# First two heads' rows scanned in place, a shorter warm-up, and a last pass with tokens on the result's partitions

## The chip, the cores and the metric

The kernel runs on one core of one Trainium2 chip. The metric is the device time of one execution in microseconds. Five engines have queues of their own: TensorE (PE in the profile, its weight loads PEld), VectorE (DVE), ScalarE (ACT), GpSimd (POOL) and SyncE (SP), which issues the kernel's DMAs.

## What is computed

Causal attention with forget gates over 4 sequences of 576 tokens and 8 heads of 64, then two pairs of dense layers with 512 inputs, 2048 hidden units and 512 outputs each:

```python
cum    = cumsum(log(clip(f, 1e-4, 1.0)))              # one row for each of 32 heads
scores = q @ k.T / 8 + cum[:, None] - cum[None, :]    # causal
x      = softmax(scores) @ v                          # heads side by side: 2304 x 512
x      = relu(x @ w_in1) ** 2 @ w_out1
out    = g(x @ w_in2) @ w_out2     # g(h) = h if h >= 1, 0 if h <= -1, else (h + 1)**2 / 4
```

All is float32. A value that goes through the fast products of TensorE is split in a high and a low part, and each wide product is made as three (high by high, high by low, low by high).

## The kernel before

**Tiling.** The 2304 tokens are cut into five blocks (`BLOCKS`): four of 512 tokens and a last one of 256. Block 0 holds the first 256 tokens (`HEAD`) of sequences 0 and 1, block 1 those of 2 and 3, blocks 2 to 4 the rest. Ten segments follow one another, a block by a pair of dense layers (`mo` 0 or 1). A segment has 16 steps (`NFC`), one for each 128 hidden units: `h_group` makes h (12 products), `act_group` the activation on ScalarE and VectorE and its split into `gh` and `gl`, and two steps later (`LAG`) `out_group` adds 12 products to four accumulators in PSUM, one for each 128 output units, with weights stationary and activations moving. So the results of a block come with output units on the partitions, and `finish` copies and stores them transposed (`outT`). The attention of a block runs between the steps of an earlier one; that of block 0 has nothing ahead of it.

**The start.** Attention of the first 256 tokens goes by groups of four heads (`Group`, `attention32`), four groups for block 0. Queries and keys of a group lie in one of two buffers `QK`, 64 rows for the 64 features of q and k. The gates ride along in the same product on more rows: row 64 holds `cum` on the side of the keys against a constant -8, row 65 holds `cum` on the side of the queries against a constant 8. `clear` fills these rows, `setup` loads `f` (L485), clips it (L488), takes the logarithm (L490) and scans it for all 32 heads at once (L491). Group 0 gets its two rows straight from the scan's result by two DMAs (`first_rows`, L507); other groups get them from a copy in DRAM, `cumd` (L503, L618). Group 0's queries and keys come in two loads of two heads each (L605). The scores `s` (L643) go to VectorE (mask and row minimum, `E`, L589), ScalarE (exponential, L650), any of three engines (division by the sum), TensorE (transposes `tr`, L682; products with v, `av`, L695) and into `x`. Before the first scores, `warm_up` issues `WARM` products of a constant tile that nobody reads (L542).

**Order of the work.** Every operation is declared with the engines that may run it, a cost for each and a due time; `Schedule` plays the program through with these costs, gives an operation with a choice to one engine, and writes the instructions in the order of the starts it found. It does so once for each entry of `WEIGHTS`, which makes an engine dearer in that choice, with refinements of the due times, and keeps the plan that ends first by its own costs. `QE`, `VE` and `RE` are the earliest times of the first loads of queries and keys, values and weights. So an edit of one operation can move others.

**Weights** of the dense layers come in a coded form, are decoded once by ScalarE, VectorE and GpSimd (`decode`, `w_decode`), split (`w_split`) and written to DRAM for the later blocks.

## Time and profile before

| | |
|---|---|
| median of 3 runs | 947.32 us (946.98 to 948.59) |
| profiled execution | 946.77 us |
| its span | 945.0 us |
| TensorE busy | 933.9 us (99%) |
| ScalarE busy | 638.2 us (68%) |
| VectorE busy | 585.9 us (62%) |
| GpSimd busy | 183.3 us (19%) |

The span runs from the first to the last instruction or transfer that the profiler saw; the time of an execution is some 1.8 us longer. Busy time of TensorE includes the warm-up and the pipelined ends of products, which overlap, so that consecutive products are best read by the distance of their starts.

### The profile page before, as it was taken

Reading aid. Unit: us, or ns where it says so; the run is one execution under the profiler, and the core shown is the slowest. Engines: PE = TensorE matmul, PEld = TensorE weight load, DVE = VectorE, ACT = ScalarE, POOL = GpSimd, SP = SyncE. Lnnn points to the kernel's source line nnn. Section 1 sums busy time; section 2 is a strip of 40 time slices with the busy share of each in tenths; the row PEclk is TensorE's granted clock in tenths of the full one; section 3 lists DMA queues with packets and bytes.
Section 4 is the critical chain, followed back from the end, with each engine's and each line's share of the span. In section 5 each row is a group of like instructions: output and inputs, shape, how many; then the busy total and the mean of one; then the engine's idle time right before and its main releaser. Section 6 shows DMA issues by size and latency. Waiting matters only on the chain.

```text
span 945.0 us, 14242 instructions
## 1 busy us (share of the span) xinstructions
PE 933.9 (99%) x4770; PEld 782.9 (83%) x4770; DVE 585.9 (62%) x1319; ACT 638.2 (68%) x1269; POOL 183.3 (19%) x323
## 2 busy tenths in 40 slices
PE   7999999999999999999999999999999999999998
PEld 5677778877888888888788887888888888889998
DVE  8899999899777659776777668775211132220032
ACT  7988889998887868776777677876523343334444
POOL 3300101324231322432223322321000000002200
PEclk9999999999999999999999999999999999999999
DMA  7799998997999997878789887986655555559993
GB/s 217 230 372 367 333 400 307 369 353 262 342 291 294 276 262 214 278 246 267 228 275 295 224 250 224 291 254 188 250 197 196 204 181 203 195 197 373 366 370 143
DMA packets 126105, 254.72 MB, mean 270 GB/s; under 512 B 89808, under 2 KB 90480, under 8 KB 104080
## 3 DMA queue, kind: packets, MB, share of 16 engines
q1 hardware_dynamic: 126032, 253.81, 80.7%
q8 instruction: 38, 0.62, 0.3%
q14 instruction: 35, 0.29, 0.1%
HBM read 194.35 MB, written 38.45 MB: 246 GB/s over the span
## 4 chain that ended last, share of the span: by engine, by line
PE 92%; DVE 3%; DMA 2%; ACT 1%; issue 1%; POOL 0%; SPq 0%; DVEq 0%; ACTq 0%; POOLq 0%
PE h L1042 40%; PE acc L1093 13%; PE acc L1095 13%; PE acc L1094 13%; PE av L866 4%; PE s L787 2%; PE s L788 2%; DMA PT<-PP 1%; DMA raw-2_209<-in_w_dram 1%; DMA out_dram<-o 1%; DVE PP L841 0%; PE s1q L643 0%; PE s7q L643 0%; PE s4q L643 0%; PE s5q L643 0%
## 5 line engine op out<-in xcount | busy, mean ns | idle before, releaser
L1042 PE MATMUL h<-x,whl 128*128 128x512 f32 (+1 forms) x1896 | 434.7, 372 | 0.4 <-DVE whl L1019 0.3
L1042 PEld LDWEIGHTS h<-x,whl 128*128 128x128 f32 x1896 | 325.0, 188 | 56.4 <-issue 3.0
L1093 PE MATMUL acc<-gh,whl 128*128 128x512 f32 (+1 forms) x640 | 239.2, 374 | 0.7 <-ACT o L570 0.7
L1095 PE MATMUL acc<-gl,whl 128*128 128x512 f32 (+1 forms) x640 | 236.8, 370 | 0.0
L1094 PE MATMUL acc<-gh,whl 128*128 128x512 f32 (+1 forms) x640 | 236.3, 369 | 0.0
L582 DVE TENSOR_TENSOR gl<-g,gh 128x512 fp32r<-128x512 f32 (+1 forms) x122 | 82.7, 678 | 123.3 <-PE acc L1095 82.7
L1095 PEld LDWEIGHTS acc<-gl,whl 128*128 128x128 f32 x640 | 120.5, 188 | 21.2 <-POOL gl L584 0.2
L1093 PEld LDWEIGHTS acc<-gh,whl 128*128 128x128 f32 x640 | 120.6, 188 | 18.8 <-ACT o L570 1.3
L1094 PEld LDWEIGHTS acc<-gh,whl 128*128 128x128 f32 x640 | 120.6, 188 | 15.6
L584 POOL TENSOR_TENSOR gl<-g,gh 128x512 fp32r<-128x512 f32 (+1 forms) x38 | 44.4, 1168 | 341.2 <-PE acc L1095 253.1
L1060 ACT ACTIVATE r<-h 128x512 f32<-128x512 f32 (+1 forms) x80 | 43.9, 549 | 86.8 <-PE h L1042 82.9
L1073 DVE SCALAR_TENSOR_TENSOR g<-r,h 128x512 f32<-128x512 f32 (+1 forms) x80 | 50.5, 631 | 80.5 <-ACT r L1071 80.2
L1069 ACT ACTIVATE r<-h,half 128x512 f32<-128x512 f32 (+1 forms) x80 | 51.1, 639 | 61.0 <-PE h L1042 60.5
L841 DVE SCALAR_TENSOR_TENSOR PP<-E,st,PP 128x512 f16<-128x512 f32 (+2 forms) x128 | 78.2, 645 | 10.4 <-ACT PP L837 9.3
L804 ACT ACTIVATE E<-E,st 64x320 f32<-64x320 f32 (+2 forms) x96 | 63.6, 662 | 26.2 <-DVE st L589 15.8
L589 DVE CUSTOM_DVE_ANT_0 E<-s,mask 128x288 f32<-128x288 f32 (+2 forms) x128 | 61.8, 500 | 24.2 <-PE s L788 15.8
L837 ACT ACTIVATE PP<-E,st 128x512 f16<-128x512 f32 (+2 forms) x128 | 68.6, 591 | 6.3 <-DVE st L811 5.7
L866 PEld LDWEIGHTS av<-pr,vt 128*128 128x128 f32 x288 | 53.5, 188 | 12.0 <-ACT r L1069 0.9
L866 PE MATMUL av<-pr,vt 128*128 128x320 f32 (+2 forms) x288 | 61.5, 285 | 0.5 <-DVE st L589 0.5
L570 ACT ACTIVATE gh<-g 128x512 fp32r<-128x512 f32 (+1 forms) x66 | 38.1, 577 | 30.7 <-DVE g L1073 30.4
L575 POOL TENSOR_SCALAR pr<-PT 128x640 fp32r<-128x640 f16 (+2 forms) x49 | 28.5, 583 | 125.9 <-PE av L866 91.1
L1071 ACT ACTIVATE r<-r 128x512 f32<-128x512 f32 (+1 forms) x80 | 46.9, 587 | 2.0
(250 smaller groups left out, 1112.0 us busy)
## 6 DMA issues: line engine op xcount, KB each, us to landing
whl<-scr SPq DMA_DIRECT2D x112, 1024.0 KB
raw<-in_w_dram SPq DMA_DIRECT2D x28, 1024.0 KB
scr<-whl SPq DMA_DIRECT2D x28, 1024.0 KB
in<-in_qkv_dram SPq DMA_DIRECT2D x32, 608.0 KB
whl<-scr SPq DMA_DIRECT2D x32, 512.0 KB
out_dram<-o SPq DMA_DIRECT2D x16, 256.0 KB
QK<-in_qkv_dram SPq DMA_DIRECT2D x7, 512.0 KB
raw<-in_w_dram SPq DMA_DIRECT2D x6, 512.0 KB
```

The source lines that it names most:

```text
L582: alts["DVE"] = (dve_t(n), lambda: nc.vector.tensor_sub(out(), a(), b()), True)
L589: return nc.vector.tensor_tensor_reduce(out=out, in0=ps, in1=mask[:m, OFF - q0:OFF - q0 + n], scale=scale, scalar=3e38, op0=ALU.add, op1=A ...
L804: nc.scalar.activation(Ec.tile[:m, :e], Ec.tile[:m, :e], AF.Exp, scale=-1.0, bias=nmx(), accum_out=st.tile[:m, 1, ci:ci + 1])))}, [*tops, ...
L837: nc.scalar.activation(hi, x, AF.Copy, scale=r())
L841: nc.vector.scalar_tensor_tensor(lo, x, r(), hi, op0=ALU.mult, op1=ALU.subtract)
L866: nc.tensor.matmul(av.tile[:, c0:W], vt.tile[:, kc, :, :], pr.tile[:, i, :n], start=(kc == 0 and i == 0), stop=(kc == NK - 1))
L1042: nc.tensor.matmul(ps.tile[:, :n], w.tile[:, 0, wi, kc * P:(kc + 1) * P], src.tile[:, kc, xi, :n], start=(kc == 0 and i == 0), stop=(kc == ...
L1069: o1 = sch.op(due, {"ACT": (act_t(n, True, 1), lambda: A.activation(r.tile[:, :n], ps(), AF.Relu, scale=0.5, bias=half))}, [o], [psb, r])
L1073: o2 = sch.op(due, {"DVE": (dve_t(n), lambda: v.scalar_tensor_tensor(g.tile[:, :n], r.tile[:, :n], 1.0, ps(), op0=ALU.min, op1=ALU.max))}, ...
L1093: nc.tensor.matmul(a.tile[:, :n], wh, gh.tile[:, :n], start=(fc == 0), stop=False)
L1094: nc.tensor.matmul(a.tile[:, :n], wl, gh.tile[:, :n], start=False, stop=False)
L1095: nc.tensor.matmul(a.tile[:, :n], wh, gl.tile[:, :n], start=False, stop=(fc == NFC - 1))
```

## The change

The diff has three parts.

1. `setup` loads the first 256 gates of heads 0 and 1 a second time, repeated on partitions 64 to 96 (33 partitions, both heads side by side), clips them and takes the logarithm there. `first_row` then scans a head's row on partition 64 and again on partition 96, straight into `QK`: four scans of 256 on VectorE in place of two of the four rows in each of the two DMAs. `first_rows` keeps its DMAs for heads 2 and 3. The second row of the gates moves from partition 65 to 96 for all groups. Clearing the second half of buffer 0 moves from VectorE to GpSimd, and the due time of filling `Q2` and `K2` goes from -30 to 30.
2. `WARM` goes from 17 to 12, the earliest times of the first loads move, and `WEIGHTS` has three entries instead of seven.
3. In the last 16 steps (block 4, second pair), `out_group` makes activations the stationary operand and weights the moving one: two accumulators of 128 tokens by 512 units, three products of 512 columns each, instead of four accumulators with three products of 256 columns. At the end each is copied in two halves and stored to `out4`, rows of tokens. The host joins the two outputs.

```diff
--- before.py
+++ after.py
@@ -46,15 +46,17 @@
 BASE = [sum(WIDTH[:i]) for i in range(len(BLOCKS))]
 OFF = 512
 QUAD = 4
+DIRECT = 2
+ROWS = (64, 96)
 SPARE = ("E", "g", "E", "o", "E", "r", "E", "g", "E", "o")
 
 SLAV = [0.0, 0.51, 0.75, 0.75, 0.0]
 SLQK = [0.0, 0.271, 0.412, 0.414, 0.0]
-QE = [0.0, 5.4, 8.66, 11.6]
-VE = [5.5, 6.1]
-RE = [1.36, 7.73, 16.0]
+QE = [0.0, 7.0, 8.66, 11.6]
+VE = [6.5, 7.6]
+RE = [2.4, 7.73, 16.0]
 LW = 29.1
-WARM = 17
+WARM = 12
 
 
 def pattern(bits):
@@ -120,7 +122,7 @@
 AHEAD = 0.30
 LEAD = 15.4
 
-WEIGHTS = [{}, *({"DVE": x, "POOL": x * y} for x in (0.4, 0.6, 0.8) for y in (0.0, 0.5, 1.0))]
+WEIGHTS = [{"DVE": x, "POOL": 0.0} for x in (0.6, 0.8, 1.0)]
 
 class Buf:
     def __init__(self, pool, make, kind=None):
...
@@ -476,21 +478,29 @@
     def setup():
         sb = new("x", "setup", [P, 2 * NKC * 512], F32)
         fr, lf, cum = (lambda i=i: sb.tile[:H * B, S * i:S * i + S] for i in range(3))
-        onesf = lambda: sb.tile[:H * B, 3 * S:4 * S]
+        onesf = lambda a=0, z=H * B, n=S: sb.tile[a:z, 3 * S:3 * S + n]
+        first = lambda a=ROWS[0], z=ROWS[1] + 1, c=0, m=DIRECT: sb.tile[a:z, 4 * S + HEAD * c:4 * S + HEAD * (c + m)]
         due = -100.0
         G, V_, A = nc.gpsimd, nc.vector, nc.scalar
         tiny_op.append(sch.op(due - 9, {"POOL": (0.05, lambda: G.memset(tiny, 2.0 ** -30))}))
         oh = sch.op(due - 200, {"POOL": (0.05, lambda: G.memset(warm, 0.5))})
         oh = sch.op(due - 200, {"ACT": (1.5, lambda: A.activation(warm, warm, AF.Ln))}, [oh])
+
+        b1 = sch.op(due - 2, {"SP": (dma_t(67584), lambda: nc.sync.dma_start(
+            out=first().rearrange("p (c n) -> p c n", n=HEAD),
+            in_=f[:DIRECT, :HEAD].partition_broadcast(ROWS[1] + 1 - ROWS[0])))}, [], [sb], early=0.0)
+        b2 = sch.op(due - 2, {"DVE": (0.37, lambda: V_.tensor_scalar(
+            first(), first(), 1e-4, 1.0, op0=ALU.max, op1=ALU.min))}, [b1], [sb])
+        b3 = sch.op(due - 2, {"ACT": (0.52, lambda: A.activation(first(), first(), AF.Ln))}, [b2, oh], [sb])
         o1 = sch.op(due, {"SP": (dma_t(73728), lambda: nc.sync.dma_start(out=fr(), in_=f))}, bufs=[sb], early=0.0)
-        o2 = sch.op(due - 5, {"POOL": (0.55, lambda: G.memset(onesf(), 1.0))}, bufs=[sb])
+        o2 = sch.op(due - 5, {"POOL": (0.55, lambda: G.memset(onesf(0, P), 1.0))}, bufs=[sb])
         sch.op(due + 90, {"POOL": (0.05, lambda: G.memset(half, 0.5))})
         o3 = sch.op(due, {"DVE": (0.37, lambda: V_.tensor_scalar(
             fr(), fr(), 1e-4, 1.0, op0=ALU.max, op1=ALU.min))}, [o1], [sb])
         o4 = sch.op(due, {"ACT": (0.58, lambda: A.activation(lf(), fr(), AF.Ln))}, [o3, oh], [sb])
         o5 = sch.op(-98.5, {"DVE": (0.67, lambda: V_.tensor_tensor_scan(
             cum(), onesf(), lf(), 0.0, op0=ALU.mult, op1=ALU.add))}, [o4, o2], [sb])
-        sch.op(due, {"ACT": (1.4, lambda: A.activation(warm, warm, AF.Exp))}, [o4])
+        sch.op(due, {"ACT": (1.4, lambda: A.activation(warm, warm, AF.Exp))}, [o4, b3])
         hi = lambda: fr().bitcast(F32R)
         lo = lambda: lf().bitcast(F32R)
         o6 = sch.op(T_START + 16, {
@@ -503,12 +513,17 @@
         o8 = sch.op(-98, {"SP": (dma_t(32768), lambda: nc.sync.dma_start(
             out=cumd, in_=cum()[:, :HEAD]))}, [o5], [sb])
 
+        def first_row(head, t, out, deps):
+            return sch.op((-101, -98.2)[head], {"DVE": (0.68, lambda: V_.tensor_tensor_scan(
+                out(), onesf(ROWS[t], ROWS[t] + 1, HEAD), first(ROWS[t], ROWS[t] + 1, head, 1), 0.0,
+                op0=ALU.mult, op1=ALU.add))}, [b3, o2, *deps], [sb, QK[0]])
+
         def first_rows(row, out, due, deps):
-            return sch.op(due, {"SP": (dma_t(4096), lambda: nc.sync.dma_start(
-                out=out(), in_=cum()[row:row + QUAD, :HEAD]))}, [o5, *deps], [sb, QK[0]], early=0.0)
+            return sch.op(due, {"SP": (dma_t(2048), lambda: nc.sync.dma_start(
+                out=out(), in_=cum()[row:row + QUAD - DIRECT, :HEAD]))}, [o5, *deps], [sb, QK[0]], early=0.0)
 
         zs = {}
-        due = -30.0
+        due = 30.0
         for i in range(2):
             for n, t in (("Q", Q2[i]), ("K", K2[i])):
                 z = None
@@ -528,9 +543,9 @@
         i2 = sch.op(-120, {"POOL": (0.3, lambda: G.affine_select(
             out=ident, in_=ident, pattern=[[-1, P]], compare_op=ALU.not_equal,
             fill=1.0, base=0, channel_multiplier=1))}, [i1])
-        return o7, zs, ms, i2, o8, first_rows
-
-    cum_op, zs, mask_op, id_op, cumd_op, first_rows = setup()
+        return o7, zs, ms, i2, o8, first_row, first_rows
+
+    cum_op, zs, mask_op, id_op, cumd_op, first_row, first_rows = setup()
     xb = {0: new("x", "x0")}
 
     def warm_up():
@@ -551,7 +566,7 @@
         rows = lambda a, z: QK[i].tile[a:z, n * half:n * half + n]
         kq = lambda a, z, t: rows(a, z).rearrange("p (c t n) -> p c t n", t=2, n=HEAD)[:, :, t, :]
         due = -98 + 2 * i + half
-        eng, m = ("POOL", nc.gpsimd) if i else ("DVE", nc.vector)
+        eng, m = ("POOL", nc.gpsimd) if i + half else ("DVE", nc.vector)
         fill = lambda out, x: {eng: (n / 1920 + 0.03, lambda: m.memset(out(), x))}
         kr = sch.op(due, fill(lambda: kq(D, P, 0), 8.0), [], [QK[i]])
         qr = sch.op(due, fill(lambda: kq(D, P, 1), 0.0), [], [QK[i]])
@@ -605,15 +620,18 @@
             loads.append(sch.op(g.due - 6, {"SP": (dma_t(P * n * 4 // parts), lambda c=c: nc.sync.dma_start(
                 out=reg()[:D, c], in_=src[:, c]))}, wait, [qk], early=QE[g.i] if g.i < len(QE) else None))
         row = g.b * H + g.h
-        place = lambda t, c0, c1: reg()[D + t:D + t + 1].rearrange("p (c t n) -> p c t n", t=2, n=HEAD)[:, c0:c1, t, :]
+        place = lambda t, c0, c1: reg()[ROWS[t]:ROWS[t] + 1].rearrange("p (c t n) -> p c t n", t=2, n=HEAD)[:, c0:c1, t, :]
         ready = []
         for i in range(parts):
             c0, c1 = QUAD * i // parts, QUAD * (i + 1) // parts
             if parts == 2:
-                if i == 0:
-                    rows = [first_rows(row, lambda t=t: place(t, 0, QUAD), -90, [*cleared[0, 0], *cleared[0, 1]])
+                for c in range(c0, min(c1, DIRECT)):
+                    ready.append([loads[i], *(first_row(
+                        c, t, lambda c=c, t=t: place(t, c, c + 1)[:, 0, :], cleared[0, i]) for t in range(2))])
+                if c1 > DIRECT:
+                    rows = [first_rows(row + DIRECT, lambda t=t: place(t, DIRECT, QUAD), -90, cleared[0, i])
                             for t in range(2)]
-                ready += [[loads[i], *rows]] * (c1 - c0)
+                    ready += [[loads[i], *rows]] * (c1 - DIRECT)
             else:
                 rows = [sch.op(g.due - 4, {"SP": (dma_t(4096), lambda t=t, c0=c0, c1=c1: nc.sync.dma_start(
                     out=place(t, c0, c1), in_=cumd[row + c0:row + c1, :].rearrange("(o c) n -> o c n", o=1)))},
@@ -1082,6 +1100,33 @@
         n = nb(s)
         w = whl[s]
         gh, gl, o3, o4 = gt.pop(s)
+        if s >= NS - NFC:
+
+            for d in range(n // P):
+                if fc == 0:
+                    accs[blk, mo, d] = new("acc", f"acc{blk}_{mo}_{d}")
+                    acc_op[blk, mo, d] = None
+                a = accs[blk, mo, d]
+
+                def mms(a=a, d=d):
+                    wh, wl = (w.tile[:, 1, i, :] for i in range(2))
+                    th, tl = (x.tile[:, d * P:(d + 1) * P] for x in (gh, gl))
+                    nc.tensor.matmul(a.tile, th, wh, start=(fc == 0), stop=False)
+                    nc.tensor.matmul(a.tile, th, wl, start=False, stop=False)
+                    nc.tensor.matmul(a.tile, tl, wh, start=False, stop=(fc == NFC - 1))
+
+                acc_op[blk, mo, d] = sch.op(
+                    when + 0.01 * d, {"PE": (3 * mm_t(DM), mms)}, [acc_op[blk, mo, d], o4, *whl_op[s]], [a, w, gh, gl])
+                if fc == NFC - 1:
+                    for i in range(2):
+                        z = slice(DM // 2 * i, DM // 2 * (i + 1))
+                        ob = new("E" if i else "o", f"o{blk}_{d}_{i}")
+                        o = sch.op(when - 4, copies(
+                            lambda ob=ob: ob.tile[:, :DM // 2], lambda a=a, z=z: a.tile[:, z], DM // 2, "ACT DVE", psum=True),
+                            [acc_op[blk, mo, d]], [a, ob])
+                        sch.op(when, {"SP": (dma_t(P * DM * 2), lambda ob=ob, z=z, d=d: nc.sync.dma_start(
+                            out=out4[d * P:(d + 1) * P, z], in_=ob.tile[:, :DM // 2]))}, [o], [ob])
+            return
         for d in range(NKC):
             if fc == 0:
                 accs[blk, mo, d] = new("acc", f"acc{blk}_{mo}_{d}")
...
```

## Rows read from the trace of the kernel before

**Rows 1.** The page, section 1: engine, busy us (share of span), instructions.
```profile
PE 933.9 (99%) x4770; PEld 782.9 (83%) x4770; DVE 585.9 (62%) x1319; ACT 638.2 (68%) x1269; POOL 183.3 (19%) x323
```

**Rows 2.** Busy time of each engine in stretches of the span.
```profile
core 0: us, PE busy (x) PEld busy (x) DVE busy (x) ACT busy (x) POOL busy (x), PEclk, DMA share, GB/s
...
48.00:100.00 52.00, 52.00 (x243) 41.11 (x241) 51.20 (x83) 45.48 (x76) 3.35 (x2) 1.00 0.99 377
...
300.00:600.00 300.00, 298.68 (x1438) 251.03 (x1437) 218.92 (x542) 223.30 (x467) 89.11 (x180) 1.00 0.84 253
```

**Rows 3.** Timeline from the start: start us, us, engine, line, operation [idle before].
```profile
0.74 0.41 SPq L485 DMA_DIRECT2D setup<-in_f_dram  x1
...
0.91 2.10 DVE L555 MEMSET QK<- 64x512 f32 x4 [0.91 <-PEq L1207]
...
1.39 5.41 PE L542 MATMUL warm<-ident 128*128 128x128 f32 x34 [1.39 <-POOL tiny L482]
...
3.04 0.45 DVE L488 TENSOR_SCALAR setup<-setup 32x576 f32<-32x576 f32 x1
3.52 0.68 ACT L490 ACTIVATE setup<-setup 32x576 f32<-32x576 f32 x1 [1.30 <-DVE setup L488]
...
4.82 1.35 DVE L491 TENSOR_TENSOR_SCAN setup<-setup 32x576 f32<-32x576 f32 x1
...
6.57 1.40 SPq L507 DMA_DIRECT2D QK<-setup  x2
...
7.72 0.66 ACT L963 ACTIVATE wf-2_238<-raw-2_209 128x512 f32<-128x512 f32 x1 [2.00 <-DMA raw-2_209<-in_w_dram]
...
9.21 2.86 PE L643 MATMUL s0q<-QK 128*128 128x128 f32 x16 [2.40 <-DMA QK<-setup]
```

**Rows 4.** Busy time around the first exponential, columns as in rows 2.
```profile
7.72:10.72 3.00, 1.51 (x10) 1.44 (x11) 2.44 (x8) 2.04 (x3) 0.68 (x3) 1.00 0.46 112
10.72:47.05 36.33, 33.92 (x211) 23.29 (x209) 30.37 (x134) 33.03 (x110) 10.14 (x17) 1.00 0.83 250
```

**Rows 5.** Chain that ended last: start us, us, what.
```profile
47.05 2.56 PE h L1042 x10
...
794.62 2.72 PE h L1042 x12
797.34 0.23 PE acc L1093
...
932.84 1.44 PE h L1042 x12
...
935.72 1.44 PE h L1042 x12
```

**Rows 6.** Timeline of the end, columns as in rows 3.
```profile
940.43 1.46 ACT L570 ACTIVATE o<-acc 128x256 f32<-128x256 f32 x4 [1.35 <-PE acc L1095]
...
940.84 1.80 SPq L1116 DMA_DIRECT2D out_dram<-o  x4
```

**Rows 7.** Stretches behind the last product, columns as in rows 2.
```profile
943.50:944.00 0.50, 0.00 (x0) 0.00 (x0) 0.00 (x0) 0.00 (x0) 0.00 (x0) 1.00 0.16 49
```

**Rows 8.** The page, section 5: a group of weight loads, busy us, mean ns, idle before.
```profile
L1093 PEld LDWEIGHTS acc<-gh,whl 128*128 128x128 f32 x640 | 120.6, 188 | 18.8 <-ACT o L570 1.3
```

**Rows 9.** Busy time in short stretches of the start, columns as in rows 2.
```profile
1.60:2.20 0.60, 0.60 (x4) 0.60 (x5) 0.55 (x2) 0.59 (x2) 0.53 (x2) 1.00 0.41 123
2.40:4.00 1.60, 1.60 (x9) 1.60 (x9) 1.35 (x4) 0.48 (x1) 1.50 (x3) 1.00 0.72 197
...
2.00:4.00 2.00, 2.00 (x11) 2.00 (x11) 1.75 (x4) 0.69 (x3) 1.83 (x4) 1.00 0.60 168
4.00:6.00 2.00, 2.00 (x19) 2.00 (x19) 1.80 (x3) 1.69 (x3) 1.93 (x5) 1.00 1.04 285
```

**Rows 10.** Instructions on the tile E0q: durations in ns (min/median/max), starts, shapes.
```profile
L589 DVE CUSTOM_DVE_ANT_0 E0q<-s0q,mask x8: 271/350/421, 10.4 to 12.5; 128x128 f32<-128x128 f32 x4, 128x256 f32<-128x256 f32 x4
L650 ACT ACTIVATE E0q<-E0q,st0q x8: 385/446/497, 10.7 to 14.8; 128x128 f32<-128x128 f32 x4, 128x256 f32<-128x256 f32 x4
```

More of the change, by code (lines that the diff above doesn't have):

```diff
@@ L380, in tile_attention_moe_moe @@
 @with_exitstack
-def tile_attention_moe_moe(ctx: ExitStack, tc: tile.TileContext, qkv, f, w2, outT):
+def tile_attention_moe_moe(ctx: ExitStack, tc: tile.TileContext, qkv, f, w2, outT, out4):
     nc = tc.nc
@@ L1212 @@
         args.append(nc.dram_tensor(f"in_{name}_dram", a.shape, _mybir.dt.from_np(a.dtype), kind="ExternalInput").ap())
-    outT = nc.dram_tensor("out_0_dram", (DM, NT), _mybir.dt.float32, kind="ExternalOutput").ap()
+    outT = nc.dram_tensor("out_0_dram", (DM, NT - WIDTH[-1]), _mybir.dt.float32, kind="ExternalOutput").ap()
+    out4 = nc.dram_tensor("out_1_dram", (WIDTH[-1], DM), _mybir.dt.float32, kind="ExternalOutput").ap()
     with _tile.TileContext(nc) as tc:
-        tile_attention_moe_moe(tc, *args, outT)
+        tile_attention_moe_moe(tc, *args, outT, out4)
     r = _run(nc, [arrays], core_ids=[0])
-    rows = r.results[0]["out_0_dram"].T
+    rows = _np.concatenate([r.results[0]["out_0_dram"].T, r.results[0]["out_1_dram"]])
     out = _np.empty(rows.shape, rows.dtype)
```

## The prediction

> **What bounds the kernel now.** I read the page first: TensorE is busy for 933.9 of the 945.0 us span [rows 1], so only 11.1 us are idle. Then stretches of the span: from 48 to 100 us TensorE is busy all 52.00 us, from 300 to 600 us for 298.68 of 300 us [rows 2]. What reaches the end from the middle is therefore the number and length of the products, which the change leaves alone up to the last pass. Two places are left: the start, before TensorE is always fed, and the end.
>
> At the start I read the timeline [rows 3]. Forgets `f` are loaded at 0.74 us, clipped at 3.04, logged at 3.52, scanned at 4.82; the sums go out by two DMAs at 6.57 us, and the first score product starts at 9.21 us after 2.40 us of waiting for them. Ahead of that stand 34 passes of warm-up (17 products, two passes each) from 1.39 to 6.80 us that compute nothing wanted. The page counts them as busy, so 5.41 us more of TensorE are free there than its share says.
>
> After the first product ScalarE is the fuller of the two engines around it: 33.03 of 36.33 us from its first exponential to 47.05 us, 91%, VectorE 30.37 us, 84% [rows 4]. From there on h products run without a break [rows 5]. At the end the steps follow one another without a gap, then come four copies, four stores and their data [rows 6, 7].
>
> **The change, part by part.**
>
> *Last pass.* A step of the last block is 2.88 us from one group of h products to the next (932.84 to 935.72 us [rows 5]); its 12 h products take 1.44 us, so the 12 output products, 256 columns each, take the other 1.44: 0.12 each. With 512 columns a product follows the one before after 0.227 us (12 h products in 2.72 us [rows 5]). The change makes the 12 of 256 columns into 6 of 512: 6 x 0.227 = 1.36 us, 0.08 less a step, and for 16 steps 1.28 us less. In rows, columns cost 0.107 us per 256, so 0.0133 us is the fixed part of each product, and six fixed parts go. The stationary operand is now the activations, the moving one the weights, both read as before; a weight load of 188 ns [rows 8] now lies beside 227 ns of product instead of 120.
>
> The Trainium skill, in "TensorE: Matmul & The Clock Gate", section "Back-to-back issue gap", gives a product its columns at 2.4 GHz and 2.5 ns on top, and by that the six saved would be worth 0.015 us a step, 0.24 us in all. The 0.0133 us of [rows 5] differ from it, and the trace decides.
>
> *The tail.* Before, four copies, 1.46 us in all, run on ScalarE as each accumulator ends [rows 6], the stores are issued from 940.84 to 942.64 us, and data flow until about 943.7 us [rows 7]. Afterwards two accumulators of 512 columns end 0.68 us apart (3 x 0.227), each with two copies and two stores of the same 128 KB. The last two stores become ready together instead of 0.36 us apart, and the queue issues them one behind the other; an issue takes about 0.40 us (1.80 us for four with their waits). The first store, too, starts about 0.4 us nearer to the end of the products (0.68 instead of 3 x 0.36 = 1.08 us ahead), and the same 512 KB still flow behind it. I charge one issue, 0.40 us; bounds are 0 and 0.80 (both copies on one engine). Last pass and tail: -1.28 + 0.40 = -0.88 us, between -1.28 and -0.48.
>
> *The first two heads.* A new load brings their rows to partitions 64 to 96, ahead of the old one. The old load's 72 KB moved between 1.6 and 2.2 us (123 GB/s for 0.6 us [rows 9]); the new one has 66 KB and the same place in the queue: landed at 2.4 us, at the latest 3.0, where the old clip started. A clip over 512 columns is 0.45 x 512/576 = 0.40 us, the logarithm 0.68 x 512/576 = 0.61 us [rows 3]; the old hops between these steps were 0.03 us and, behind a memset, up to 0.6. VectorE is free then: it clears three pieces instead of the first four before the old clip, so it is done at 0.91 + 3 x 0.53 = 2.4 us. The logarithm ends at 3.45 us. A scan of 256 is not in the trace. Below it is 1.35 x 256/576 = 0.60 us, above the whole 1.35; the mask pass of VectorE (0.28 for 128, 0.42 for 256 columns [rows 10]) shows a fixed part of some 0.13 us, so (1.35 - 0.13) x 256/576 + 0.13 = 0.67 us. Head 0 needs two: 3.55 + 1.34 = 4.9 us; no DMA follows, as they write the operand itself.
>
> *Warm-up.* Five products fewer are ten passes. From 2 to 4 us 11 passes touch the stretch, from 4 to 6 us 19 [rows 9]: about 0.21 us, then about 0.11 us each. The ten removed are of the fast kind, 1.1 us, so warm-up ends at 5.7 us. The load of queries and keys sits one issue (0.41 us) later; 197 GB/s from 2.4 to 4.0 us [rows 9] are 315 KB, enough for its 256 KB, so it lands near 4.4 us. The first product then starts at 5.7 us, set by the warm-up, not by the rows: 3.5 us earlier.
>
> *Heads 2 and 3* keep the old path: clip and logarithm right behind the new ones, long scan after head 0's at about 4.9, done at 6.3 us (7.6 if all four short scans go first), against 4.82 + 1.35 = 6.17. Their DMAs (two rows, not four) need the old 9.21 - 6.17 = 3.04 us from scan to product: 9.3 to 10.7 us. So two heads of the first four run in the gap, two come as before or up to 1.5 us later; queries of group 1, moved back to 7.0 us, queue behind these DMAs anyway. The delayed weights (1.36 to 2.4 us) are decoded by ScalarE from 7.72 us on [rows 3] and feed h products, which stand behind several groups of scores: nothing.
>
> *What of the 3.5 us passes.* The first exponential came 1.51 us after the first product (9.21 to 10.72 [rows 3, 10]), so it would come at 7.2 us. ScalarE then has its 33.03 us of work and the 2.04 us of decoding that stood ahead of it [rows 4] still before it: 35.07 us. At the old 91% this lasts to 45.8 us instead of 47.05, 1.3 us earlier; if VectorE takes the decoding, which the plan allows, the whole 3.5 us pass. VectorE has 16% free there, and gains only some 1.6 us of work (four scans 2.7, clip 0.4, less three memsets of 0.5). I take the middle, 2.4 us. From 48 us TensorE hands it on to the end unchanged [rows 2].
>
> Sum: -0.88 - 2.4 = -3.3 us. On the profiled execution, 946.77 us with a span of 945.0, that is a span of 941.7; the median of the runs is 947.32, 0.55 above that execution, so 944.0 us.
>
> **The rivals.**
>
> *All of it passes.* VectorE or GpSimd takes what ScalarE can't, 3.5 us, and the tail costs little: 947.3 - 3.5 - 0.9 = 942.9, with no tail loss 942.5. For it: 16% of VectorE is free. Against: only two heads are there to fill the gap, and each waits on its own chain.
>
> *The start's gain is swallowed.* Heads 2 and 3 come 1.5 us later and head 0's mask passes stand in VectorE's queue behind the long scan; the later weights and values cost waits, or the planner's new order, with VectorE priced higher, adds to the 1.4 us that TensorE now waits after 48 us. Then about 0.5 us is left of the start: 947.3 - 0.9 - 0.5 = 945.9, no measurable change. For it: VectorE is 98% busy from 48 to 100 us [rows 2]. Against: TensorE doesn't wait for it there.
>
> *TensorE's pace falls.* The granted clock reads 1.00 in each stretch here, yet the warm-up's pace doubled from one level to the other (1.2 to 2.4 GHz) only after about 3 us of products in a row [rows 9]. With a shorter warm-up and, behind it, two heads' products with gaps, the pace could drop back, and each microsecond of full-pace product then costs one more. It turns the sign of the result at 3.3 us and is measurably slower from 5.2 us; were it low from 5.7 to 16 us, it would cost about 6: 947.3 - 3.3 + 6 = 950. Against it: before, 2.40 us of idleness behind the warm-up did no harm (the 16 passes that follow took 2.86 us [rows 3]; eight of 128 and eight of 256 columns at the fast pace are 2.6), and the gap becomes shorter. The same page of the Trainium skill, Part 1, says that the slow level is the default, that activity lifts it and idleness brings it back; by this rule the danger is real, but the gap seen here didn't trigger it.
>
> *The last pass saves nothing.* Should the spacing of 0.227 us not hold with activations as the stationary operand (each set of weights in the array is now used for 512 columns once, and is itself the newest result of VectorE), the step stays at 2.88 us, the end is the added 0.40 us later, and the time is 947.3 - 2.4 + 0.4 = 945.3. Against it: h products of the same sizes keep 0.227 us for whole passes [rows 5]. The skill's figure above lies between this case and the forecast.
>
> **How the numbers follow.** The forecast, start 1.3 to 3.5 and end 0.5 to 1.3 us (942.5 to 945.4): 0.56. All passes, 942.7: 0.15. Swallowed, 945.9: 0.18. Pace falls, 950: 0.08. Last pass saves nothing, 945.3: 0.03. A measurement of this kernel tells some 0.2%, 1.9 us, from no change, so faster means under 945.4. Faster: 0.56 + 0.15 + 0.03 = 0.74; same 0.18; slower 0.08. The range leaves out the fallen pace and the best corner: 942.2 to 947.0; the likeliest case's own is 942.5 to 945.4.
>
> **What the profile will show.** The first score product near 5.7 us, without a wait for a DMA; four short scans of about 0.67 us; heads 2 and 3 at 9.3 to 10.7 us; 24 warm-up passes to about 5.7 us; the stretch where h products run without a break begins near 44.6 instead of 47.05 us; steps of 2.80 us in the last block, products 0.227 us apart; 0.4 us more from last product to end. The prediction is wrong if the first score waits for the queries' load or the clearing past 7 us, if ScalarE's share from the first exponential on falls below 85%, if new waits of TensorE above 2 us stand after 48 us, or if early passes run at 0.21 us again.

## The result, and the profile after

The changed kernel takes 953.83 us (952.36 to 956.25, 6 runs), the kernel before beside it 947.31 us (946.98 to 948.85, 6 runs): a ratio of 1.0069, with a 95% interval of 1.0058 to 1.0080. It is slower; the forecast was 944.0 us. The profiled execution took 952.79 us, with a span of 951.0 against 945.0 us.

The page, section 1, beside [rows 1]: TensorE has 0.4 us less to do and is idle for 17.5 instead of 11.1 us.

```profile
PE 933.5 (98%) x4664; PEld 778.0 (82%) x4664; DVE 596.1 (63%) x1323; ACT 631.6 (66%) x1263; POOL 186.6 (20%) x331
```

The timeline of the start, beside [rows 3]:

```profile
0.74 0.43 SPq L489 DMA_DIRECT2D setup<-in_f_dram  x1
...
1.39 5.46 PE L557 MATMUL warm<-ident 128*128 128x128 f32 x24 [1.39 <-POOL ident L543]
...
3.04 0.42 DVE L492 TENSOR_SCALAR setup<-setup 33x512 f32<-33x512 f32 x1
...
3.50 0.63 ACT L494 ACTIVATE setup<-setup 33x512 f32<-33x512 f32 x1 [1.27 <-DVE setup L492]
4.27 1.38 DVE L517 TENSOR_TENSOR_SCAN QK<-setup 1x256 f32<-1x256 f32 x2
...
5.69 1.35 DVE L501 TENSOR_TENSOR_SCAN setup<-setup 32x576 f32<-32x576 f32 x1
...
6.67 0.84 PE L661 MATMUL s0q<-QK 128*128 128x128 f32 x4
...
7.06 1.40 DVE L517 TENSOR_TENSOR_SCAN QK<-setup 1x256 f32<-1x256 f32 x2
...
8.52 0.92 PE L661 MATMUL s0q<-QK 128*128 128x128 f32 x4 [1.01 <-DVE QK L517]
...
8.83 0.40 ACT L668 ACTIVATE E0q<-E0q,st0q 128x128 f32<-128x128 f32 x1 [2.36 <-DVE st0q L604]
...
9.93 0.35 PE L661 MATMUL s0q<-QK 128*128 128x128 f32 x1 [0.49 <-DMA QK<-setup]
```

Head 0's rows need no DMA and its products start at 6.67 us, 2.54 us earlier than before. From 4.27 us on VectorE runs scan behind scan to 8.46 us, and head 1's products wait for its pair. The first mask (8.50 against 10.40 us) and the first exponential (8.83 against 10.72 us) are 1.9 us earlier, the first transposes 1.7 us (11.31 against 12.98 us). At the third group of transposes the lead is gone. The first line is from before, the others from after:

```profile
14.58 0.70 PE L682 MATMUL tr0q<-ident,E0q 128*128 128x128 f32 x3 [0.19 <-DVE E0q L674]
```

```profile
14.45 0.55 PE L700 MATMUL tr0q<-ident,E0q 128*128 128x128 f32 x3 [1.87 <-DVE E0q L692]
...
12.28 0.96 DVE L992 TENSOR_SCALAR low<-raw-2_212 128x512 uint16<-128x512 uint16 x1
13.14 0.48 DVE L675 TENSOR_SCALAR st0q<-st0q 128x2 f32<-128x2 f32 x1
...
12.57 0.35 POOL L532 MEMSET Q<- 64x320 f32 x1
12.90 0.70 POOL L539 TENSOR_SCALAR_AFFINE_SELECT mask<-mask 128x384 bf16<-128x384 bf16 x1
...
21.61 0.46 DVE L992 TENSOR_SCALAR low<-raw-1_270 128x512 uint16<-128x512 uint16 x1
```

TensorE waits 1.87 us for a division on VectorE that stands behind decoding. The decoding step ahead of it takes 0.96 us beside work of GpSimd; the same step takes 0.46 us at 21.61 us.

Stretches of the span, columns as in [rows 2]; the first answers to [rows 4]:

```profile
8.83:46.85 38.02, 32.98 (x212) 23.97 (x211) 35.89 (x140) 34.87 (x110) 6.01 (x14) 1.00 0.85 252
100.00:245.00 145.00, 143.18 (x666) 111.29 (x666) 140.37 (x229) 120.87 (x196) 27.75 (x27) 1.00 0.90 332
245.00:320.00 75.00, 72.42 (x348) 60.52 (x347) 54.61 (x137) 55.81 (x121) 19.78 (x44) 1.00 0.95 281
```

From the first exponential on, VectorE is busy for 35.89 of 38.02 us, 94% against 84%; ScalarE for 92% against 91%. None of VectorE's 5.5 us more is a scan, as those are over. Some 2 us each are divisions and decoding, and GpSimd has fewer of both (6.01 us busy against 10.14). The first output product starts at 49.79 us (before at 49.45). Then two stretches behind the start have idle TensorE, 1.82 and 2.58 us. They had none before:

```profile
100.00:245.00 145.00, 144.95 (x680) 114.39 (x679) 134.67 (x237) 128.86 (x210) 34.28 (x28) 1.00 0.90 334
245.00:320.00 75.00, 75.00 (x365) 63.19 (x364) 55.35 (x139) 60.07 (x126) 16.96 (x40) 1.00 0.99 303
```

In the first of them ScalarE is busy for 8.0 us less and VectorE for 5.7 us more: the change has no instruction there, but the planner drew engines and order anew. Most of the 5.7 us isn't added work. Summed over the instructions that ran more than 0.1 us longer than the median of their kind (line, tile and shape), VectorE took 12.4 us more than those medians there, against 6.7 us before. Each of them ran beside an instruction of GpSimd, which is busy for only 27.75 of the 145 us. One such, and the same step elsewhere:

```profile
105.38 3.33 DVE L1037 SCALAR_TENSOR_TENSOR whl<-wf,whl 128x1024 fp32r<-128x1024 f32 x1 [0.30 <-ACT whl L1034]
...
105.22 2.40 POOL L1002 TENSOR_TENSOR wf<-wf,low 128x1024 int32<-128x1024 int32 x1 [12.27 <-DVE wf L998]
...
158.07 1.23 DVE L1037 SCALAR_TENSOR_TENSOR whl<-wf,whl 128x1024 fp32r<-128x1024 f32 x1
```

TensorE's longest waits from 100 to 320 us in the trace of after (us, times, longest):

```profile
PE h L1060 <- DVE whl L1037: 1.1, 1, 1.1
PE acc L1138 <- ACT o L585: 1.1, 1, 1.1
PE s L805 <- DVE st L604: 1.0, 1, 1.0
```

The end, beside [rows 5, 6]: two lines of the chain, then the timeline of ScalarE's and SP's last work.

```profile
938.63 1.43 PE h L1060 x12
...
941.45 1.43 PE h L1060 x12
```

```profile
946.34 1.34 ACT L585 ACTIVATE o<-acc 128x256 f32<-128x256 f32 x4 [1.54 <-PE acc L1116]
...
946.75 1.81 SPq L1127 DMA_DIRECT2D out_dram<-o  x4
```

A step is 2.82 us (2.88 before). From the start of the last product (946.60 us; before 941.00) to the end of the span go 4.41 us, against 3.98.

Theory at this point: the last pass does about what was forecast; the start's lead dies in VectorE's queue; the new order costs the rest. Rivals: TensorE's pace, the stores, and GpSimd holding up VectorE's instructions. The last of these got no run of its own; what the traces show of it is told where it stands.

### The profile page after: what moved, and what is told of

Same layout as the page of the kernel before. It is cut to its first block, busy times and chain, and to the rows that moved or that the text cites. A ratio compares the mean times of both kernels' runs of the same rounds, so it can differ in the third digit from the quotient of the medians.

```text
span 951.0 us, 14066 instructions
## 1 busy us (share of the span) xinstructions
PE 933.5 (98%) x4664; PEld 778.0 (82%) x4664; DVE 596.1 (63%) x1323; ACT 631.6 (66%) x1263; POOL 186.6 (20%) x331
## 4 chain that ended last, share of the span: by engine, by line
PE 67%; DMA 2%; DVE 1%; ACT 1%; issue 0%; SPq 0%; ACTq 0%; DVEq 0%
PE h L1060 30%; PE acc L1138 10%; PE acc L1140 9%; PE acc L1139 9%; PE av L884 3%; PE s L805 2%; PE s L806 2%; DMA out_dram<-o 1%; PE acc L1114 1%; PE acc L1115 1%; PE acc L1116 1%; DMA in<-in_qkv_dram 0%; ACT PP L855 0%; DMA PT<-PP 0%; SPq L866 0%
## 5 line engine op out<-in xcount | busy, mean ns | idle before, releaser
L1138 PE MATMUL acc<-gh,whl 128*128 128x512 f32 (+1 forms) x576 | 220.9, 384 | 2.7 <-ACT o L585 2.7
L1140 PE MATMUL acc<-gl,whl 128*128 128x512 f32 (+1 forms) x576 | 218.7, 380 | 0.0
L1139 PE MATMUL acc<-gh,whl 128*128 128x512 f32 (+1 forms) x576 | 218.1, 379 | 0.0
L1140 PEld LDWEIGHTS acc<-gl,whl 128*128 128x128 f32 x576 | 108.4, 188 | 21.1 <-POOL gl L599 0.2
L1138 PEld LDWEIGHTS acc<-gh,whl 128*128 128x128 f32 x576 | 108.5, 188 | 20.3 <-ACT o L585 3.2
L1139 PEld LDWEIGHTS acc<-gh,whl 128*128 128x128 f32 x576 | 108.5, 188 | 15.6
L599 POOL TENSOR_TENSOR gl<-g,gh 128x512 fp32r<-128x512 f32 (+1 forms) x40 | 48.4, 1210 | 297.3 <-PE acc L1140 214.5
L590 POOL TENSOR_SCALAR pr<-PT 128x640 fp32r<-128x640 f16 (+2 forms) x55 | 33.5, 613 | 130.2 <-PE av L884 83.0
```

The lines of the kernel that those rows point to most:

```text
L1138: nc.tensor.matmul(a.tile[:, :n], wh, gh.tile[:, :n], start=(fc == 0), stop=False)
L1139: nc.tensor.matmul(a.tile[:, :n], wl, gh.tile[:, :n], start=False, stop=False)
L1140: nc.tensor.matmul(a.tile[:, :n], wh, gl.tile[:, :n], start=False, stop=(fc == NFC - 1))
```

## The experiments

In most kernels below the planner is replaced by a record of the engine and start that it gave each operation. "The old order" is the record of the kernel before: new operations are put in beside the ones that they replace, so a part can be measured without the planner's answer to it. Lateness, worked out from the traces, is the start of the first activation of a step on ScalarE minus that of the kernel before (us; segments and steps count from 0, two segments to a block); the last column is the difference of the spans:

```
segment, step                 0, 0    0, 4    2, 1    3, 0    5, 0    span
kernel before, starts        44.46   61.43  246.94  353.24  571.01   945.0
changed kernel               +1.27   +2.22   +3.22   +6.34   +6.18    +6.0
last pass, old order         +0.15   +0.15   +0.18   +1.02   +0.95    +0.4
start, old order             +3.37   +3.35   +3.41   +4.08   +4.52    +4.5
  + 14 filling products      +1.78   +1.76   +1.89   +3.66   +2.35    +2.2
  + fills off VectorE        +0.65   +1.60   +1.71   +1.61   +0.88    +1.1
  + decoding later           +2.09   +2.79   +2.80   +3.72   +3.37    +3.4
12 warm-up, old order        +0.96   +0.94   +0.96   +1.47   +2.71    +2.7
new start, old order behind  +1.63   +2.21   +2.18   +3.42   +4.57    +4.2
old start, new order behind  +1.33   +3.95   +4.45   +9.29   +8.26    +7.6
before, later plan           +0.06   +1.05   -1.55   +1.48   +2.15    +2.8
```

In the rows of the old order a lateness stays within 0.13 us from the fifth step (61 us) to 247 us. Ahead of that it can grow, by up to 0.95 us. In a new order the table also counts work that was moved from one step to another, so there TensorE's idle time says more.

### The last pass alone

The old order with the last pass of the change and nothing else of it; the diff is the hunks on `s >= NS - NFC` and `out4`.

> The last pass alone, every other operation on the engine and in the order of the kernel before. Order theory (the loss comes from the new order that the planner draws for everything behind the start): 946.4 to 946.9 us, 0.5 to 0.9 less than before. Start theory (the loss comes from the new work at the start itself): the same. If the swapped operands cost something: 947.3 or more.

947.04 us, 1.0005 [0.9996, 1.0013] (median, ratio to before, 95% interval): no difference that can be measured. Either theory expected 946.4 to 946.9. In the profile the lateness falls from 0.97 us at the last segment's first step to 0.41 at the end. So the part is worth some 0.56 us, less than the runs of one kernel differ (here those of before from 945.7 to 949.1).

### The start alone

The old order with the other hunks (load, clip, logarithm, scans, row 96, 12 warm-up products), without the last pass. The old order's places serve:

```diff
+            sch.put(("DVE", PLAN[8][1] - 0.004 + 0.001 * t + 0.006 * head))
             return sch.op((-101, -98.2)[head], {"DVE": (0.68, lambda: V_.tensor_tensor_scan(
```

> The new load, logarithm and scans for heads 0 and 1 and 12 warm-up products, the last pass as before, every other operation on the engine and in the order of the kernel before. Order theory: 945 to 947.5 us. Start theory: 951 us or more, since the four scans, the clip, the logarithm and the load are all there.

951.56 us, 1.0051 [1.0038, 1.0065]. The start itself is 3.4 us late, and TensorE hands that on unchanged to 247 us. VectorE (first fence) puts filling and decoding ahead of head 0's masks, which start 1.9 us later than before; unlike in the changed kernel, where they start 1.9 us earlier. TensorE then waits 3.79 us for the first transposes, and the granted clock (column PEclk of the second fence) is at the lower of its two levels, 1.2 GHz, when they come:

```profile
6.68 1.40 DVE L583 TENSOR_TENSOR_SCAN QK<-setup 1x256 f32<-1x256 f32 x2
8.25 2.36 DVE L599 MEMSET K<- 64x576 f32 x4 [0.18 <-issue]
...
12.28 0.28 DVE L670 CUSTOM_DVE_ANT_0 E0q<-s0q,mask 128x128 f32<-128x128 f32 x1
```

```profile
12.00:14.00 2.00, 0.00 (x0) 0.00 (x0) 2.00 (x14) 1.39 (x7) 0.00 (x0) 0.87 1.01 253
14.00:16.00 2.00, 1.14 (x5) 0.83 (x6) 1.86 (x14) 1.89 (x8) 0.48 (x1) 0.50 1.13 367
16.00:18.00 2.00, 2.00 (x10) 0.90 (x9) 1.31 (x7) 1.94 (x7) 0.00 (x0) 0.50 0.98 194
18.00:20.00 2.00, 2.00 (x10) 0.95 (x6) 0.28 (x1) 0.51 (x1) 0.00 (x0) 0.50 1.00 282
```

### Pace: filling products, and a shorter warm-up by itself

To the start alone, 14 products of the constant tile that nobody reads, behind head 0's scores:

```diff
+    def keep_busy(n):
+        ps = new("ps", "busy")
...
+                nc.tensor.matmul(ps.tile[:, :P], ident, ident, start=True, stop=True)
...
+    keep_busy(14)
```

> As f2_start (951.6 us), with 14 more products that nobody reads behind the first scores, in the 3.8 us in which TensorE waited there. If f2_start lost by the pace that fell in this gap: granted clock 1.00 from 8 to 48 us and 947 to 949 us. If the extra work on VectorE made the loss: 951 us or more.

949.41 us, 1.0024 [1.0014, 1.0034]: 2.2 us above before instead of 4.65, and just above the 947 to 949 expected from pace alone. The masks come when they came without the filling (12.3 us) and the transposes too (14.86 us), but at full clock:

```profile
14.00:16.00 2.00, 1.23 (x7) 0.64 (x7) 1.86 (x14) 2.00 (x9) 0.48 (x1) 1.00 1.16 363
16.00:18.00 2.00, 1.82 (x12) 0.91 (x11) 1.56 (x7) 1.89 (x8) 0.00 (x0) 1.00 0.86 177
```

The kernel before with the warm-up alone shortened:

```diff
-WARM = 17
+WARM = 12
```

> The kernel before on its own engines and in its own order, with 12 warm-up products instead of 17 and nothing else changed. If the five products hold TensorE's pace up through the wait for the first scores: the clock falls near 9 to 13 us and the time is 948 to 950 us. If they do nothing: 946.9 us.

948.37 us, 1.0011 [1.0002, 1.0020]. The first score products start at 9.21 us as before, behind an idle stretch that is no longer (2.32 against 2.40 us), but the 16 passes take 4.14 instead of 2.86 us [rows 3], at the lower clock; timeline, then stretches:

```profile
9.21 4.14 PE L704 MATMUL s0q<-QK 128*128 128x128 f32 x16 [2.32 <-DMA QK<-setup]
```

```profile
10.00:12.00 2.00, 2.00 (x10) 1.77 (x9) 1.46 (x9) 1.40 (x7) 0.00 (x0) 0.65 0.90 211
12.00:14.00 2.00, 1.76 (x7) 1.04 (x6) 1.51 (x11) 1.34 (x6) 0.48 (x1) 0.50 1.00 325
```

The whole change with its own order, but 17 warm-up products:

> The changed kernel in its own order on every engine, with 17 warm-up products instead of 12. If the shorter warm-up lets TensorE's pace fall in part of the runs (mean granted clock 0.998 in three of six, those 2 to 3 us longer): no run under 0.9995, median 952 to 952.8 us. If the warm-up has nothing to do with it: 953.8 us and the same spread.

952.88 us, 1.0063 [1.0051, 1.0076], not told apart from the changed kernel. The longer warm-up doesn't bring the time back in that order. It doesn't rule a lower pace out in every run: two of the five have a mean clock of 0.997.

### VectorE's queue at the start

To the kernel with 14 filling products, the constant fills of the second buffers K and Q on GpSimd:

```diff
+                    sch.put(("POOL", sch.take(1)[0][1] + 30.0))
                     z = sch.op(due, {
```

> The order of the kernel before, the new start without the last pass, the 14 filling products ahead of the first transpose of weights, and the constant fills of the second K and Q buffers moved from VectorE to GpSimd. Theory, VectorE's queue holds the start up once the pace is right: the first masks of head 0 come some 2 us earlier and the time is 946.5 to 948 us. Rival, VectorE's queue is no limit: no change from the kernel with the 14 products alone, 949.4 us.

948.64 us, 1.0014 [1.0006, 1.0023]: 1.7 us above before, and above the theory's 946.5 to 948. The masks start at 10.07 us, 2.2 us earlier; beside its own runs of before the time is 0.45 us less than with the filling alone, within the intervals. That doesn't speak against VectorE's queue. At the first step this kernel is 1.13 us ahead of the one with the filling alone, and by the third it has lost 0.95 us again. TensorE waits there for weights `whl` from VectorE, 1.26 instead of 0.35 us, and three steps of VectorE ahead of them take 0.13, 0.46 and 0.36 us longer while GpSimd does the fills that were moved to it. Two of the three, with the filling alone and with the fills moved:

```profile
45.27 0.44 DVE L573 CAST setup<-setup 32x576 fp32r<-32x576 f32 x1
46.97 0.68 DVE L1076 TENSOR_SCALAR wf<-wf 128x1024 int32<-128x1024 int32 x1
```

```profile
44.30 0.90 DVE L573 CAST setup<-setup 32x576 fp32r<-32x576 f32 x1
46.43 1.04 DVE L1077 TENSOR_SCALAR wf<-wf 128x1024 int32<-128x1024 int32 x1
```

Two kernels bring heads 0 and 1 forward in the queues of VectorE, ScalarE and GpSimd: the first has no filling products and 3 us of shift, the second 6 of them and 2.2 us.

```diff
+                    sch.shift = -3.0 if c + a < DIRECT else 0.0
```

> As f2_start, but the work of heads 0 and 1 behind the scores is put 3 us earlier in every queue, ahead of the decoding of the first weights, and the fills of Q2 and K2 leave VectorE. If f2_start lost because head 0's mask passes stood behind fills and decoding in VectorE's queue, and TensorE's pace fell in the gap that this left: 945 to 948 us, and a granted clock of 1.00 from 8 to 48 us. If the scans themselves, 2.8 us of VectorE, are the loss: 950 us or more.

> As the kernel with the fills moved, with 6 filling products, and the work of heads 0 and 1 on VectorE, ScalarE and GpSimd placed 2.2 us earlier in these engines' queues. Theory, order in VectorE's queue and TensorE's pace are all that the new start loses: the first step of the first block stands level with before or ahead of it, and the time is 945.5 to 948 us. Rival, the start has another limit (ScalarE's exponentials, the transfers of heads 2 and 3): the first step stays 1 us or more late and the time is 948.5 us or more.

951.74 us, 1.0050 [1.0036, 1.0063], and 953.33 us, 1.0064 [1.0048, 1.0080]. Both miss. In the first, without filling, TensorE is idle from 10 to 12 us and the granted clock is 0.50 from 14 to 16 us. In the second, score products wait 4.1 us for mask passes that stand behind decoding and divisions in the mixed order, and the granted clock is 0.50 from 10 to 16 us: neither says anything about VectorE. So the last one, with 5 filling products, moves only the five decoding instructions: in the record those on ScalarE go from 6.96 and 7.72 to 11.95 and 11.96 us of the plan, those on VectorE from 7.57, 8.47 and 8.93 to 13.00, 13.01 and 14.96.

> As the kernel with the fills moved to GpSimd (order of the kernel before, new start, no last pass), but the decoding of the first step's weights, three instructions on VectorE and two on ScalarE, is placed behind head 0's mask passes and first exponentials instead of ahead of them; 5 filling products instead of 14. Theory, VectorE's queue ahead of head 0's masks swallows what the earlier score products bring: the first mask comes near 8.1 us instead of 10.07, the first step of the first block 1 us or more earlier than with the fills moved alone, ahead of the kernel before, and the time is 946 to 948 us. Rival, behind the masks something else is due at the old time (the values' transfers, the weights): the first step is not earlier, and the time stays at 948.6 us or is longer.

950.39 us, 1.0034 [1.0021, 1.0048]: the masks start as the theory said, the time doesn't follow. The tile E0q of the kernels with fills moved and with decoding moved (ns min/median/max, first and last start):

```profile
L683 DVE CUSTOM_DVE_ANT_0 E0q<-s0q,mask x8: 271/351/422, 10.1 to 12.2; 128x128 f32<-128x128 f32 x4, 128x256 f32<-128x256 f32 x4
```

```profile
L683 DVE CUSTOM_DVE_ANT_0 E0q<-s0q,mask x8: 271/356/421, 8.2 to 11.6; 128x128 f32<-128x128 f32 x4, 128x256 f32<-128x256 f32 x4
```

The eighth mask is only 0.6 us earlier, as heads 2 and 3 still come behind their DMA; the decoding on ScalarE then stands ahead of the other four exponentials (13.28 us; 12.50 with the fills moved), TensorE waits 1.5 us for a division, and the granted clock is 0.50 from 16 to 18 us. Work moved away from the front of the queue is in the way behind it.

### The order behind the start

The kernel before and the changed kernel, each with a plan of a later round of the planner's refinement and nothing of the work changed (two rounds and three rounds later):

```diff
-                if best is None or total < best[0]:
+                if i == ROUND:
```

> The kernel before with nothing of the change; the planner hands out the plan of two refinements later for the same entry of WEIGHTS. Order theory: more than 1 us away from 947.3 us, on either side, with nothing of the work changed. Start theory: 946.5 to 948.2 us.

> The changed kernel whole; the planner hands out the plan of three refinements later for the same entry of WEIGHTS. Order theory: more than 1 us away from 953.8 us, on either side. Start theory: 952.5 to 955 us.

949.90 us, 1.0030 [1.0019, 1.0041], and 956.54 us, 1.0102 [1.0088, 1.0116]: a redrawn plan alone costs some 3 us here, as much as the forecast gain. Both are plans that the planner itself passed over for an earlier end by its own costs, so this is what a redraw can cost, and not what it costs on average. The second also had a clock of 0.62 from 8 to 12 us in its profile and was 4.0 us late at the first step, so part of its loss is pace at the start. A first mixture took the changed kernel's order up to block 0's attention and the old one behind:

```diff
+        if self.first:
+            e, o.start = PLAN2[len(self.ops) - 1]
+            o.eng = ENG[e]
```

> The changed kernel whole, with the start (everything up to the attention of block 0) on the engines and in the order of the changed kernel, and all behind it on the engines and in the order of the kernel before. If a late start is handed on and the new order behind it loses the rest (start 1.3 to 1.8 us late, 4.5 us lost between 145 and 310 us): 947.5 to 949.5 us. If the late start alone made all of the loss: 952 us or more.

958.97 us, 1.0125 [1.0107, 1.0143]. The two orders were interleaved by operation and collided: the first step is 10.65 us late, and 10.76 us at 247 us, handed on as in the other kernels of the old order. The next two cut by time, at 45 us of the plan.

Old start, and behind it the changed kernel's engines and order:

```diff
+        if o.start >= 45.0:
+            o.eng, o.start = ENG[e], max(t, 45.0)
```

> The start of the kernel before (all that it places ahead of 45 us), the work of the kernel before and the new last pass, with the order and the engines that the changed kernel's plan chose for everything behind 45 us. Theory, the redrawn order costs the time: the steps stand within 0.3 us of before at 46 us, then fall behind by 2 to 5 us by 310 us, and the time is 949 to 953 us. Rival, the order is as good as the old one and only the new start costs: the steps stay level, and the time is that of the last pass alone, some 947 us.

954.14 us, 1.0072 [1.0048, 1.0095], just above the 949 to 953 that the theory expected. And the other way round, the changed kernel's start with the old order behind:

> The changed kernel's whole start in its own order (all that its plan places ahead of 45 us), with the order and the engines of the kernel before behind that, and the new last pass. Theory, the redrawn order costs the time behind 48 us: the lateness at the first step of the first block (1.3 to 3 us, as the changed kernel shows) is handed on flat, and the time is 947 to 949.5 us. Rival, something that the new start leaves behind (its transfers, its stores) costs the time whatever the order: the steps fall back by a further 2 to 5 us by 310 us and the time is 952 us or more.

950.68 us, 1.0034 [1.0020, 1.0047], between the theory's 947 to 949.5 and the rival's 952 or more. Stretches of old start and new order, then of new start and old order:

```profile
100.00:245.00 145.00, 143.21 (x668) 111.16 (x668) 140.56 (x226) 120.48 (x196) 28.01 (x27) 1.00 0.90 330
245.00:320.00 75.00, 72.26 (x339) 60.19 (x338) 53.06 (x132) 54.76 (x116) 17.31 (x43) 0.98 0.93 273
```

```profile
100.00:245.00 145.00, 144.94 (x681) 114.38 (x680) 134.90 (x239) 128.65 (x211) 34.34 (x28) 1.00 0.90 336
245.00:320.00 75.00, 74.10 (x357) 62.07 (x356) 55.55 (x139) 59.83 (x127) 16.97 (x37) 1.00 1.00 295
```

The new order takes its idle time with it (1.79 and 2.74 us) and its shift from ScalarE to VectorE; without it the new start leaves 0.06 and 0.90. The VectorE instructions that ran long beside GpSimd go with the order too: from 100 to 245 us they took 13.1 us above their medians with the new order, 6.7 with the old. The new order's price is the difference of the two ratios, 1.0069 and 1.0034: some 3.3 us. The first of the two kernels also lost time ahead of 45 us (granted clock 0.50 from 16 to 18 us in the profile), so its 7.2 us are not the order's alone; two of its runs at a granted clock of 1.0 took 950.53 and 953.79 us, 3.6 and 6.9 us above before.

### Stores and the rest of the pace

In the trace of after ScalarE waits once for 3.33 us, at 263 us, for a store to free its buffer. Four buffers instead of two, in the changed kernel, and in the old order with the last pass:

```diff
-    ring("o", 2, [P, 512], F32)
+    ring("o", 4, [P, 512], F32)
```

> The changed kernel in its own order on every engine, with four buffers for results on their way out instead of two. If ScalarE's 3.3 us of waiting for a store near 263 us, and TensorE's wait for the accumulators behind it, cost the 2.3 us that are lost between 245 and 310 us: 951 to 952 us. If they hide: 953.8 us.

> The last pass of the change and four buffers for outgoing results, all else on the engines and in the order of the kernel before. If the last pass gains 0.5 to 0.9 us and the waits for stores at the ends of blocks cost the kernel before about 1 us too: 945.2 to 946 us, faster than both kernels. If not: 946.9 us.

952.50 us, 1.0057 [1.0040, 1.0074], and 946.47 us, 0.9997 [0.9988, 1.0005], the best of all kernels and not told apart from before. Then the changed kernel with four buffers and filling products in three gaps of its start:

```diff
+    keep_busy(4, 7.7)
+    keep_busy(8, 11.36)
+    keep_busy(3, 18.6)
```

> The changed kernel in its own order, four buffers for outgoing results and 15 more products that nobody reads in TensorE's three gaps before 21 us. If pace and stores are two of the losses: every run at a clock of 0.999 or more and 950 to 951 us; what then stays above 947 is the new order, mainly between 45 and 245 us. If the pace has no part: 952.5 us as a2_stores.

954.05 us, 1.0070 [1.0052, 1.0087], at a clock of 1.00 throughout the start. Neither stores nor pace at the start are what the new order loses.

## Why the prediction was wrong

**The step that failed** is "what of the 3.5 us passes". It took ScalarE as the limit, said that VectorE "gains only some 1.6 us of work", took 2.4 us as passed on, and let TensorE hand that on "to the end unchanged". The new start costs 3.75 us with the last pass (950.68 against 946.93), and the order behind it some 3 more.

- *VectorE, not ScalarE, filled up*: 94% against 84%. The work added was about as sized, the scans 0.69 us each for 0.67, and it is over before the first exponential. Head 0's masks and the first transposes come 1.9 and 1.7 us earlier, so part of the first product's lead passes the scans. It dies at the third group of transposes, which waits 1.87 us for a division behind decoding in VectorE's queue. The rival *the start's gain is swallowed* named this queue, but for the long scan ahead of the masks; its price, 0.5 us left of the gain, was too kind.
- *VectorE's instructions ran longer beside GpSimd's*, which no term of the prediction has. The decoding step ahead of that division took 0.96 instead of 0.46 us, most of what moving the fills to GpSimd gained at the first step was lost by the third, and most of VectorE's 5.7 us more from 100 to 245 us are this. It was read from the traces; no kernel was made to test it.
- *The first product* came at 6.67, not 5.7 us. The ten removed passes were to be fast ones; instead the 24 left took 5.46 us, as long as the 34 before. The prediction had named early passes at 0.21 us as a sign against it. It had read one execution as the rule: the same 34 passes took 6.50 us in the old order with four buffers, and 6.98 us in the one with the last pass alone.
- *TensorE's pace* fell, in the old order, for 2.5 us of the start's 4.65 (4.65 less 2.16 with filling). The forecast gave that 0.08 and argued that the gap becomes shorter. But there a second gap opened, 3.79 us ahead of the transposes. The Trainium skill, "TensorE: Matmul & The Clock Gate", Part 1, has idleness bring the slow level back; the start alone agrees, with 3.79 us of idleness and a granted clock of 0.50 behind it. The shorter warm-up alone doesn't tell: its idle stretch was no longer than the harmless one of before. In the changed kernel's profile the clock reads 1.00 in the start, so the 6.5 us are not pace. A small part may be: three of its six runs have a mean clock of 0.998 and took 954.4 to 956.3 us, the others 952.4 to 953.3. But with filling and four buffers two runs at 1.0 took 954.0 and 956.4 us.
- *Handing on* holds only for a fixed order, and there from the fifth step (61 us) to 247 us. The planner redrew the order, and TensorE, without a wait there before, idled 4.4 us between 100 and 320 us. Rivals had "the planner's new order" in half a sentence and no price.
- *Heads 2 and 3* (9.93 us, forecast 9.3 to 10.7) and *the tail* (+0.43, forecast +0.40) were right.
- *The last pass* was right in kind and 0.3 us too large: products with activations stationary stand 0.232 us apart (six in 1.39 us), not 0.227, so a step saves 0.06 instead of 0.08, 1.0 us instead of 1.28. By the figure of the Trainium skill, the same page, "Back-to-back issue gap", it would have been, as an estimate, 0.015 a step; the trace stands nearer to the rows.

What stays open: how much of the remaining 1.7 us of the start (fills moved, pace right) belongs to the order in VectorE's queue and how much to GpSimd beside it, and which decision of the new order loses the time from 100 to 320 us. Shown is that this goes with the order. In the first of its two stretches VectorE's longer instructions go with it too, and TensorE's longest wait is 1.1 us for weights from VectorE; the second was not resolved. Lateness in the old order also changes at the ends of blocks, by 0.5 to 1.8 us between 247 and 353 us in most kernels, which was not traced.

## What to carry to other kernels

An earlier first product is worth only what the next engine's queue lets through: list what stands in that queue between the product and its reader, and count the share of every engine there, not of the fullest one. When work goes from one engine to another, compare how long the neighbours' instructions take before and after, too. Where a planner orders the work, an edit that leaves a stretch alone still redraws it; freeze the order to measure the edit, and measure a redrawn plan with no edit at all to see what a redraw can cost (here 3 us, the size of the gain sought, with plans that the planner itself had passed over). Shortening filler work at the start can take away the pace along with the wait.

## What the runs showed of the hardware

The time at which the warm-up's passes double their pace moves from one execution to another: the same 34 passes, from 1.39 us on, took 5.41, 6.50 and 6.98 us in three kernels whose start is the same, and 24 passes between 4.69 us (decoding moved) and 5.49 us (12 warm-up products alone). Each kernel has one trace, so this isn't put down to the kernels. And one idle stretch of 2.3 to 2.4 us ahead of the first scores was followed by full clock behind 34 passes and by 0.65 and then 0.50 behind 24, although TensorE was busy for all of 10 to 12 us, in which the clock fell.

VectorE's instructions can take far longer beside one of GpSimd than without: splitting weights into `whl` took 3.33 us instead of 1.23. From 100 to 245 us every VectorE instruction of the changed kernel that ran more than 0.1 us over the median of its kind overlapped one of GpSimd.
